# Up products on 384 tokens, with a PSUM bank for each half, in the last two sequences of an attention and mixture kernel

## The chip, the cores and the metric

The kernel runs on one core of a Trainium2 chip. The metric is the device time of one execution in microseconds (us); the time before is 678.16 us, the median of three runs (678.03 to 678.35). The engines named below are PE (TensorE, the matrix multiplier; PEld is its weight load, which runs beside the multiplying), DVE (VectorE), ACT (ScalarE), POOL (GpSimd) and SP (SyncE, which here only issues DMAs).

## What is computed

A local attention with summary keys feeds a gated projection. Cut to what matters:

```python
# q, k, v: (4 sequences, 8 heads, 768 tokens, 64); all float32
k_sum = k.reshape(B, H, 24, 32, D).max(axis=3)
v_sum = v.reshape(B, H, 24, 32, D).mean(axis=3)
scores_l = q @ k^T / 8, kept where |i - j| < 16, else -1e9
scores_s = q @ k_sum^T / 8 + log(32)
a = softmax(concat(scores_l, scores_s))
x = (a @ concat(v, v_sum))            # 3072 tokens x 512
out = ((x @ w_a) * (x @ w_b)) @ w_out # w_a, w_b: 512 x 1536, w_out: 1536 x 512
```

## The kernel before

**The projection.** The 1536 hidden columns are 12 blocks of 128 (index `f`), and the 3072 tokens are 12 chunks of 256 (index `u`, three to a sequence). One pair of a chunk and a block is an item (`item`, L1001): 144 items in all. To keep float32 accuracy every operand is held as a high and a low part, and a product is three products of parts (high with high, high with low, low with high). So the up product of one half (`up`, L981; half a with `w_a`, half b with `w_b`) is 4 slices of the 512 inputs times 3 part pairs, 12 matmuls with 128 x 128 weights standing in the array and 256 tokens of x streaming (L987). An item has 24 of them. Then a chain of four short steps: ACT copies half a out of PSUM (`g`, L1013), DVE multiplies half b by it (L1016), ACT rounds the product to its high part (`gh`, L1018), DVE subtracts that to get the low part (`gl`, L1021). The down product (`down`, L1027, matmuls L1031) then takes `gh` and `gl` as weights, 128 tokens at a time, with 512 columns of `w_out` streaming: for each of the chunk's two token tiles two matmuls with `gh` and one with `gl`, 6 per item, summed over f in the banks o0 and o1.

**PSUM.** There are 8 banks of 512 float32 columns. Both halves of an item share one bank, 256 columns each, and items alternate between h0 and h1 (`pa, pb = bank[hk][:, :CH], bank[hk][:, CH : 2 * CH]`). o0 to o3 hold outputs, c0 and c1 serve the attention. After the third chunk, o2 and o3 also serve the attention, and its token tiles alternate between (c0, c1) and (o2, o3) (L914 and L915).

**The attention.** It runs beside the projection, two chunks ahead, one tile of 128 tokens at a time (`attention`, L908): scores on PE (L617), mask and row maximum on DVE (L642, L650), exponentials on ACT (L662), normalisation on POOL (L692), twelve 32 x 256 transposes on DVE (L736), the product with the values on PE (L750), and a split of the result into the high and low part of x on ACT (L758) and DVE (L761). Per sequence, `prep_keys` (L486) builds the keys and `prep_values` (L528) the value summaries: loads of v, adds on POOL (L545), and small DMAs that put the sums into another layout (`S<-S` in the trace) and from there beside the values (`vw<-S`). The value product of a sequence's first tile needs them.

**Order.** Nothing loops at run time. Every operation is entered into `Work` (L44) with a rank, a duration and what it reads and writes; `emit` (L74) walks through modelled time and writes each engine's program in the resulting order: of the operations whose inputs are there, the one of lowest rank. `ORDER` (L23) corrects ranks and start times by the number of the operation, for operations 3 to 626. Each engine then runs its program strictly in that order and waits on semaphores. The down product of an item has the rank n - 0.5, so that it comes after the up product of the next item where its inputs are not there earlier. The four chain steps have the rank 0 and come first where they are ready.

Of the kernel before, what the change touches and what calls it, by code (L numbers as in the profile page):

```python
# [9 lines left out]
F32 = mybir.dt.float32  # L10
F32R = mybir.dt.float32r
# [97 lines left out]
def attention_moe(  # L109
# [10 lines left out]
    nc = tc.nc  # L120
# [11 lines left out]
    NR = S // CH  # L132
    NU = NR * B
    G = CH // P
    CV = 512
# [70 lines left out]
    xs = [[sb([P, NP, CH], f"x{i}_{p}", F32R) for p in range(2)] for i in range(2)]  # L206
    gs = [sb([P, CH], f"g{i}") for i in range(2)]
    ghs = [sb([P, CH], f"gh{i}", F32R) for i in range(2)]
    gls = [sb([P, CH], f"gl{i}", F32R) for i in range(2)]
# [9 lines left out]
    spaces = {n: sb([P, 2048], n) for n in ("S0", "S1")}  # L219
# [4 lines left out]
    kins = [kin, spaces["S1"][:, 2 * CV : 2 * CV + S + 32]]  # L224

# [40 lines left out]
    def rank_of(u):  # L266
        return FIRST if u == 0 else NEXT if u < FILL else SOON if u == FILL else LATER
# [134 lines left out]
    vsums = {}  # L402

# [7 lines left out]
    def blocks(rank, key, dst, x, b, c, row, more=()):  # L411
# [6 lines left out]
        for h in range(2):  # L418
            for e in range(D // 32):
# [6 lines left out]
                for rows, m in spans:  # L426
                    load(
                        rank, 4 * m, 95, more, [f"{key}.{r0}"],
# [57 lines left out]
    def prep_keys(b):  # L486
        rank = PREP
        work.add("-", 0, 0, 0, (), ["S1.2", "S1.3"], lambda: None)
        more = ["done12"], ["S1.2", "S1.3"]
        for c in range(NP):  # L490
            kw = kins[c % 2]
            keys = blocks(96, f"kin{c % 2}", kw, k, b, c, -16, more[c % 2])
# [35 lines left out]
    def prep_values(b):  # L528
# [3 lines left out]
        rank = LATER  # L532
        vs, vk = slot("S0", 2)
        work.add("-", 0, 0, 0, (), [vk], lambda: None)
        vs = vsums[b] = vs[:NS].rearrange("p (h d) -> p h d", d=D)

        vm, pk = spaces["S1"][: 4 * NS, 4 * CV - D :], "vm"
        work.add("-", 0, 0, 0, ["S1.3"], [pk], lambda: None)
        x = spaces["S1"][: 4 * NS, : 2 * T * D]
        keys = ["S1.0", "S1.1"]  # L540
# [7 lines left out]
        for hg in range(2):  # L548
            vv = v[b, 4 * hg : 4 * hg + 4].rearrange("h (n t) d -> (h n) t d", t=BLK)
            for i in range(BLK // T):  # L550
                load(
                    100, 197.0, 150, (), [keys[i % 2]],
                    slot("S1", i % 2)[0][: 4 * NS].rearrange("p (t d) -> p t d", d=D),
                    vv[:, i * T : (i + 1) * T, :],
                )
                if i % 2:
                    n = T * D
# [3 lines left out]
                    if i == 1:  # L561
                        add(n, vm, x[:, :n], x[:, n : 2 * n], keys + [pk])
                    else:
                        add(n, x[:, :n], x[:, :n], x[:, n : 2 * n], keys)
                        add(n, vm, vm, x[:, :n], keys + [pk])
            pool(
                rank, 0.3, (), [pk],
                lambda: nc.gpsimd.tensor_scalar(
                    out=vm, in0=vm, scalar1=1.0 / BLK, scalar2=None, op0=ALU.mult
                ),  # L570
            )
            for h in range(4):
                load(
                    99, 6.0, 20, [pk, vk], [f"{vk}.{hg}.{h}"],
                    vs[:, 4 * hg + h, :], vm[h * NS : (h + 1) * NS, :],
                )
        return [f"{vk}.{hg}.{h}" for hg in range(2) for h in range(4)]
# [15 lines left out]
    def scores(u, t, qT, qk, s, sk, banks, diag=None, lead=None):  # L593
        kind = 0 if t == 0 else 2 if t == S // P - 1 else 1
        rank = rank_of(u) + (0.2 * (t % G) if u < FILL else 0)
# [42 lines left out]
        for h in range(2):  # L638
            if not masked:
# [14 lines left out]
        for h in range(2):  # L654
            l = m[:, 1, h, :]
# [42 lines left out]
    def transposes(u, t, s, sk, banks, diag=None):  # L698
        rank = rank_of(u)
# [28 lines left out]


        for i, kb in enumerate(((0, 1, 3), (1, 2, 3), (0, 1, 2), (1, 2, 3))):  # L730
            qs = slice(32 * i, 32 * (i + 1))
            for j in kb:
                js = slice(32 * j, 32 * (j + 1))
                dve(
                    rank, 0.45, sk + ["S0.2"] * own, [f"{key}{i}{j}"],
# [412 lines left out]
```

## Time and profile before

| what | value |
|---|---|
| median of 3 runs | 678.16 us (678.03 to 678.35) |
| the profiled execution's own time | 678.28 us |
| its span, first to last instruction | 676.5 us |
| outside the span | 1.8 us |
| PE busy | 657.0 us, 97% of the span |
| DVE busy | 434.4 us, 64% |
| ACT busy | 255.4 us, 38% |
| POOL busy | 186.8 us, 28% |
| granted TensorE clock, mean | 0.999 of full speed (2.4 GHz) |

The profile is of one execution. A busy share tells how much of the span an engine had work in flight, and a busy PE is not yet a PE at its best rate: matmuls overlap in the pipeline, so the rate is read from the distance between the starts of successive groups, not from the duration of one. Idle time of an engine counts only where PE waits for it. In slices of one fortieth of the span (16.9 us) DVE is busy 7 to 9 tenths in the first 330 us and 2 tenths in the last 100 us, PE 9 tenths in all slices but the first three and the last.

### The profile page before, as it was taken

The numbers are of one execution on the slowest core, as the hardware profiler recorded it, in microseconds if no ns is written. First come the engines' busy times: TensorE is split into PE (matmuls) and PEld (weight loads), VectorE is DVE, ScalarE is ACT, GpSimd is POOL, SyncE is SP. The second block draws the span as 40 slices with busy tenths as digits, with TensorE's granted clock in tenths as the row PEclk, the third lists the DMA queues.
The fourth block names the chain that finished last, engine by engine and source line by source line (L and its number), as shares of the span: only waits on it lengthen the run. The fifth ranks groups of instructions, "written<-read, shape, count | busy, mean of one in ns | idle before, by whom it ended". The sixth has DMA issues, their size and how long they took to land.

```text
span 676.5 us, 15121 instructions
## 1 busy us (share of the span) xinstructions
PE 657.0 (97%) x5988; PEld 620.7 (92%) x5988; DVE 434.4 (64%) x989; ACT 255.4 (38%) x797; POOL 186.8 (28%) x231
## 2 busy tenths in 40 slices
PE   6889999999999999999999999999999999999997
PEld 4679989899999999999999999999999999999996
DVE  4799999996757768777665776762772762322222
ACT  4996665533323333234332332332332432211211
POOL 6678979851533310413110101110110110000000
PEclk9999999999999999999999999999999999999999
DMA  9999863266224135532311330310310100000000
GB/s 226 264 284 238 266 169 126 41 137 137 67 78 112 49 56 103 96 61 80 57 25 28 75 57 15 77 25 1 87 25 1 56 22 1 33 1 1 32 1 32
DMA packets 155087, 54.84 MB, mean 81 GB/s; under 512 B 132472, under 2 KB 148088, under 8 KB 155016
## 3 DMA queue, kind: packets, MB, share of 16 engines
q1 hardware_dynamic: 154872, 53.74, 33.5%
q8 instruction: 47, 0.77, 0.5%
q14 instruction: 24, 0.20, 0.1%
q10 hardware_dynamic: 144, 0.13, 0.1%
HBM read 47.12 MB, written 6.29 MB: 79 GB/s over the span
## 4 chain that ended last, share of the span: by engine, by line
PE 77%; DVE 11%; SPq 3%; ACT 3%; issue 2%; DMA 2%; POOL 1%; DVEq 0%; ACTq 0%; POOLq 0%
PE h L987 47%; PE o L1031 23%; SPq L260 3%; DVE c L339 2%; PE c L750 2%; PE c L617 2%; PE o L750 1%; DVE pt L736 1%; ACT s L662 1%; DVE space L345 1%; PE o L617 1%; DVE S L345 1%; DVE space L332 1%; DMA space<-in_v_dram 1%; DVE S L332 1%
## 5 line engine op out<-in xcount | busy, mean ns | idle before, releaser
L987 PEld LDWEIGHTS h<-x,w 128*128 128x128 f32 x3456 | 405.0, 192 | 6.8 <-DVE x L761 0.6
L987 PE MATMUL h<-x,w 128*128 128x256 f32 x3456 | 406.7, 275 | 0.3 <-DVE x L761 0.3
L1016 DVE TENSOR_TENSOR h<-h,g 128x256 f32<-128x256 f32 x144 | 61.9, 430 | 148.9 <-ACT g L1013 147.6
L1031 PE MATMUL o<-w,gh 128*128 128x512 f32 x576 | 151.8, 386 | 1.4 <-ACT gh L1018 1.3
L1013 ACT COPY g<-h 128x256 f32<-128x256 f32 x144 | 53.6, 372 | 256.4 <-PE h L987 256.3
L1031 PEld LDWEIGHTS o<-w,gh 128*128 128x128 f32 x576 | 103.6, 197 | 12.1 <-ACT gh L1018 2.6
L692 POOL TENSOR_TENSOR s<-s,nml 128x512 f32<-128x512 f32 x40 | 41.6, 1041 | 233.1 <-DVE nml L677 232.6
L736 DVE STREAM_TRANSPOSE pt<-s 32x256 f32<-32x256 f32 x228 | 99.4, 436 | 7.1 <-POOL s L692 2.0
L1031 PE MATMUL o<-w,gl 128*128 128x512 f32 x288 | 86.3, 381 | 0.0
L1021 DVE TENSOR_TENSOR gl<-h,gh 128x256 fp32r<-128x256 f32 x144 | 60.4, 419 | 30.6 <-ACT gh L1018 29.3
L662 ACT ACTIVATE s<-s,nml 128x128 f32<-128x128 f32 x160 | 62.2, 391 | 44.9 <-DVE nml L650 44.9
L1018 ACT CAST gh<-h 128x256 fp32r<-128x256 f32 x144 | 53.5, 371 | 65.3 <-DVE h L1016 65.1
L1031 PEld LDWEIGHTS o<-w,gl 128*128 128x128 f32 x288 | 55.9, 196 | 6.1 <-issue 0.3
L545 POOL TENSOR_TENSOR S<-S 96x64 f32<-96x64 f32 (+3 forms) x54 | 35.2, 651 | 41.6 <-DMA S<-in_v_dram 30.7
L324 ACT ACTIVATE c<-raw 128x512 f32<-128x512 f32 x36 | 26.9, 748 | 13.1 <-DVE S L332 6.6
L662 ACT ACTIVATION_READ_ACCUMULATOR s<-s,nml 128x1 f32 x160 | 30.1, 188 | 0.0
L382 POOL TENSOR_TENSOR space<-space,w 128x1024 f32<-128x1024 f32 (+1 forms) x14 | 26.8, 1915 | 8.8 <-ACT w L377 6.6
L671 DVE TENSOR_SCALAR nml<-nml 128x4 f32<-128x4 f32 x40 | 9.6, 243 | 28.4 <-ACT s L662 28.4
L388 POOL TENSOR_TENSOR w<-space 128x1024 fp32r<-128x1024 f32 (+1 forms) x14 | 26.7, 1912 | 1.0
L650 DVE TENSOR_REDUCE nml<-s 128x4 f32<-128x512 f32 x40 | 25.3, 667 | 0.0
L444 POOL COPY kT<-ksum 128x144 f32<-128x144 f32 x16 | 4.7, 308 | 62.8 <-DVE ksum L522 48.0
L382 POOL TENSOR_TENSOR S<-S,w 128x512 f32<-128x512 f32 (+1 forms) x11 | 17.4, 1582 | 6.4 <-ACT w L377 6.4
(109 smaller groups left out, 460.6 us busy)
## 6 DMA issues: line engine op xcount, KB each, us to landing
raw<-in_moe_w_a_dram SPq DMA_DIRECT2D x12, 512.0 KB
raw<-in_moe_w_b_dram SPq DMA_DIRECT2D x12, 512.0 KB
raw<-in_moe_w_out_dram SPq DMA_DIRECT2D x12, 512.0 KB
out_dram<-S SPq DMA_DIRECT2D x23, 256.0 KB
qin<-in_q_dram SPq DMA_DIRECT2D x160, 32.0 KB
S<-in_v_dram SPq DMA_DIRECT2D x24, 192.0 KB
vw<-in_v_dram SPq DMA_DIRECT2D x18, 192.0 KB
kin<-in_k_dram SPq DMA_DIRECT2D x24, 100.0 KB
```

Of the source, the lines that this page charges most:

```text
L324: nc.scalar.activation(bank["c0"], high[:, :, 1].bitcast(F32), AF.Prelu, scale=2.0**-112, alpha=-(2.0**32))
L382: lambda ms=ms, f8=f8: nc.gpsimd.tensor_tensor(out=f8, in0=f8, in1=parted(0)[:, ms].bitcast(F32), op=ALU.subtract),
L545: lambda: nc.gpsimd.tensor_tensor(out=out, in0=i0, in1=i1, op=ALU.add),
L662: lambda h=h, c=c, sums=sums: nc.scalar.activation(s[h][:, c, :], x[h][:, c, :], AF.Exp, bias=m[:, 0, h, c : c + 1], scale=1.0, accum_out= ...
L692: lambda h=h, r=r: nc.gpsimd.tensor_tensor(out=s[h], in0=s[h], in1=r[:, :, None].broadcast_to([P, NP, P]), op=ALU.mult,),
L736: lambda js=js, qs=qs: nc.vector.transpose(out=pv[js, :, qs], in_=sv[qs, :, js]),
L987: nc.tensor.matmul(ps, w[:, c, part, :], x[xpart][:, c, :].rearrange("p (a b) -> p b a", a=G), start=(i == 0), stop=(i == n - 1),)
L1013: act(CHAIN, 0.38, [hk], [gk], lambda: nc.scalar.copy(out=g, in_=pa))
L1016: lambda: nc.vector.tensor_tensor(out=pa, in0=pb, in1=g, op=ALU.mult),
L1018: act(CHAIN, 0.41, [hk], [ghk], lambda: nc.scalar.copy(out=gh, in_=pa))
L1021: lambda: nc.vector.tensor_tensor(out=gl, in0=pa, in1=gh.bitcast(F32), op=ALU.subtract),
L1031: nc.tensor.matmul(bank[ok[j]], (gh if first else gl)[:, j::G], w[:, :, part, :].rearrange("p (z a) n -> p z n a", a=2), start=(f == 0 and ...
```

## The change

The chunks of the third and fourth sequence become 384 tokens (`WIDE = 3` tiles of 128), two to a sequence instead of three: 10 chunks instead of 12. In these chunks

- an up matmul streams 384 columns instead of 256;
- half a fills the bank h0 and half b the bank h1, and the two halves are two entries of the plan instead of one; the chain multiplies into half b's bank; there is one buffer of `g`, `gh`, `gl` of 384 columns instead of two of 256;
- a down product covers three tiles: 9 matmuls into o0, o1 and o2. The attention therefore keeps c0 and c1 for scores and o3 for value products, from the second sequence on;
- q is loaded a tile at a time (4 DMAs of half the size per tile instead of 16 per two tiles).

In all chunks x now lies in one tile of 9 slots (`xt`), stored so that the matmul's interleaved read steps by 64 columns instead of 128; the split (L802 and after) reads PSUM with a step of 2 for it, and `gh` and `gl` are read as weights without a step. The value sums of a sequence have their own small tile (`vm`); those of the third and fourth sequence are prepared from one buffer instead of two. Ranks after the third chunk go by sequence and tile. In the very last item half b of the up product is placed between the two parts of the previous item's down product.

```diff
-    NR = S // CH
-    NU = NR * B
+    WIDE = 3
+    chunks = [(b, t, n) for b, n in enumerate((G, G, WIDE, WIDE)) for t in range(0, S // P, n)]
+    NU = len(chunks)
...
-    xs = [[sb([P, NP, CH], f"x{i}_{p}", F32R) for p in range(2)] for i in range(2)]
+    xt = sb([P, 9, NP, P], "x", F32R)
...
+    vm = sb([P, 2, D], "vm")
...
-    def rank_of(u):
-        return FIRST if u == 0 else NEXT if u < FILL else SOON if u == FILL else LATER
+    def rank_of(u, t=None):
+        if u > FILL:
+            b, t0, _ = chunks[u]
+            return LATER + 2 * b + 0.2 * (t0 if t is None else t)
+        return FIRST if u == 0 else NEXT if u < FILL else SOON
...
+        at, keys, rank = (0, ["S1.0", "S1.1"], LATER) if b == 1 else (3, ["S1.3"], 50)
...
-                    100, 197.0, 150, (), [keys[i % 2]],
+                    90, 197.0, 150, (), [keys[j]],
...
-        if u > FILL:
-            banks, vbank = [["c0", "c1"], ["o2", "o3"]], ["c0", "o2"]
+        banks, vbank = ["c0", "c1"], ["c0", "c1"] if u == FILL else ["o3"] * n
...
-                    x[xpart][:, c, :].rearrange("p (a b) -> p b a", a=G),
+                    inputs_of(u, xpart)[:, :, c].rearrange("p g (a b) -> p g b a", a=2),
...
+            W = m * P
+            ghk, glk = "gh0", "gl0"
+            pa, pb, g, gh, gl = bank["h0"][:, :W], bank["h1"][:, :W], gt[:, :W], ght[:, :W], glt[:, :W]
+            for nm, ps, hk in (("a", pa, "h0"), ("b", pb, "h1")):
+                pe(
+                    n - (1.45 if n == total - 1 and nm == "b" else 0), 12 * (0.112 if m == 2 else 0.163), xk + weight_key(f, nm), [hk],
+                    lambda nm=nm, ps=ps: up(nm, f, u, ps),
+                )
+            act(CHAIN, 0.13 + W / 1030, ["h0"], ["g0", "g1"], lambda: nc.scalar.copy(out=g, in_=pa))
+            dve(
+                CHAIN, 0.08 + W / 1000, ["g0", "h1"], ["h1"],
+                lambda: nc.vector.tensor_tensor(out=pb, in0=pb, in1=g, op=ALU.mult),
+            )
+            act(CHAIN, 0.16 + W / 1030, ["h1"], [ghk], lambda: nc.scalar.copy(out=gh, in_=pb))
...
-                        bank[ok[j]], (gh if first else gl)[:, j::G],
+                        bank[ok[j]], (gh if first else gl)[:, j * P : (j + 1) * P],
```

**Where the order moves.** Up to the score product of the second sequence's first tile, the five engines' programs have the same order. Three places after that follow. In them h_75 and h_76 are the banks h0 and h1, o_71 to o_74 the banks o0 to o3, c_77 and c_78 the attention's banks, a name w with a number is a slot of weights, and x2 or x12 is the count of equal instructions in a row.

PE in the third sequence, an item in the steady state; before, the up product of one item and the down product of the item ahead of it (the 24 up matmuls of an item are rows like the first three, and here are its last):

```order
L987 MATMUL h_75<-x_0_171,w_1477 128x256 x2
L987 MATMUL h_75<-x_1_172,w_1477 128x256
L987 MATMUL h_75<-x_0_171,w_1477 128x256
L1031 MATMUL o_71<-w_1384,gh_176 128x512 x2
L1031 MATMUL o_72<-w_1384,gh_176 128x512 x2
L1031 MATMUL o_71<-w_1384,gl_178 128x512
L1031 MATMUL o_72<-w_1384,gl_178 128x512
```

and after:

```order
L1037 MATMUL h_76<-x,w_558 128x384 x12
L1037 MATMUL h_75<-x,w_665 128x384 x12
L1108 MATMUL o_71<-w_558,gh 128x512 x2
L1108 MATMUL o_72<-w_558,gh 128x512 x2
L1108 MATMUL o_73<-w_558,gh 128x512 x2
L1108 MATMUL o_71<-w_558,gl 128x512
L1108 MATMUL o_72<-w_558,gl 128x512
L1108 MATMUL o_73<-w_558,gl 128x512
L1037 MATMUL h_76<-x,w_665 128x384 x12
```

Between an item's half b (bank h1) and its down product now stands half a of the next item, 12 matmuls, where the 24 matmuls of a whole item stood.

SP, from the loads of q for the second sequence's tiles 2 and 3 to the value sums of that sequence; before:

```order
L260 DMA qin<-in_q_dram 32x8x32 x16
L260 DMA S_187<-in_v_dram 96x512 x4
L260 DMA S_186<-S_187 24x64 x4
L260 DMA vw_165<-S_186 24x512
L260 DMA vw_166<-S_186 24x512
```

and after:

```order
L288 DMA S_181<-in_v_dram 96x512 x3
L288 DMA qin<-in_q_dram 32x8x32 x9
L288 DMA S_181<-in_v_dram 96x512
L288 DMA qin<-in_q_dram 32x8x32 x7
L288 DMA S_182<-vm 24x64 x4
L288 DMA vw_165<-S_182 24x512
L288 DMA S_181<-in_v_dram 96x512
L288 DMA vw_166<-S_182 24x512
```

The last loads of v for this sequence went ahead of the loads of q, and a load for the third sequence stands in the middle of them. On PE the value product that reads `vw` stood behind the up product of the tenth hidden block of the third chunk; it now stands earlier, between the high and the low part of the down product of the seventh block, with one more score product (of tile 2) ahead of it.

PE, the end of the program; before:

```order
L987 MATMUL h_76<-x_0_171,w_1614 128x256
L1031 MATMUL o_71<-w_1558,gh_175 128x512 x2
L1031 MATMUL o_72<-w_1558,gh_175 128x512 x2
L1031 MATMUL o_71<-w_1558,gl_177 128x512
L1031 MATMUL o_72<-w_1558,gl_177 128x512
L1031 MATMUL o_71<-w_1614,gh_176 128x512 x2
L1031 MATMUL o_71<-w_1614,gl_178 128x512
L1031 MATMUL o_72<-w_1614,gh_176 128x512 x2
L1031 MATMUL o_72<-w_1614,gl_178 128x512
```

and after:

```order
L1037 MATMUL h_76<-x,w_1609 128x384
L1108 MATMUL o_71<-w_1553,gl 128x512
L1108 MATMUL o_72<-w_1553,gl 128x512
L1108 MATMUL o_73<-w_1553,gl 128x512
L1108 MATMUL o_71<-w_1609,gh 128x512 x2
L1108 MATMUL o_72<-w_1609,gh 128x512 x2
L1108 MATMUL o_71<-w_1609,gl 128x512
L1108 MATMUL o_72<-w_1609,gl 128x512
L1108 MATMUL o_73<-w_1609,gh 128x512 x2
L1108 MATMUL o_73<-w_1609,gl 128x512
```

Between the last up matmul and the last down product stood 6 matmuls of the item before; now stand the 3 with its low part.

## Rows read from the trace of the kernel before

**Rows 1.** The page: span, busy time and share, chain that ended last by engine

```profile
span 676.5 us, 15121 instructions
PE 657.0 (97%) x5988; PEld 620.7 (92%) x5988; DVE 434.4 (64%) x989; ACT 255.4 (38%) x797; POOL 186.8 (28%) x231
PE 77%; DVE 11%; SPq 3%; ACT 3%; issue 2%; DMA 2%; POOL 1%; DVEq 0%; ACTq 0%; POOLq 0%
```

**Rows 2.** Stretches: length, busy us (instructions) of PE, PEld, DVE, ACT, POOL, clock, DMA

```profile
575.10:622.80 47.70, 47.70 (x361) 46.22 (x360) 11.89 (x27) 9.84 (x27) 0.00 (x0) 1.00 0.04 12
416.70:469.10 52.40, 52.40 (x490) 50.20 (x489) 29.80 (x70) 16.64 (x60) 4.17 (x4) 1.00 0.17 37
```

**Rows 3.** Timeline of one steady item: start, us, engine, line, operation, [idle before]

```profile
602.94 2.84 PE L987 MATMUL h<-x,w 128*128 128x256 f32 x24
...
605.62 1.03 PE L1031 MATMUL o<-w,gh 128*128 128x512 f32 x4
605.87 0.37 ACT L1013 COPY g<-h 128x256 f32<-128x256 f32 x1 [2.74 <-PE h L987]
...
606.28 0.43 DVE L1016 TENSOR_TENSOR h<-h,g 128x256 f32<-128x256 f32 x1 [2.68 <-ACT g L1013]
...
606.75 0.37 ACT L1018 CAST gh<-h 128x256 fp32r<-128x256 f32 x1 [0.50 <-DVE h L1016]
606.92 2.84 PE L987 MATMUL h<-x,w 128*128 128x256 f32 x24
```

**Rows 4.** Groups by line and shape: busy us, mean ns | idle before

```profile
L1016 DVE TENSOR_TENSOR h<-h,g 128x256 f32<-128x256 f32 x144 | 61.9, 430 | 148.9 <-ACT g L1013 147.6
L1018 ACT CAST gh<-h 128x256 fp32r<-128x256 f32 x144 | 53.5, 371 | 65.3 <-DVE h L1016 65.1
L642 DVE SCALAR_TENSOR_TENSOR s<-c,mask 128x512 f32<-128x512 f32 x22 | 14.3, 685 | 2.8 <-PE c L617 2.8
L758 ACT CAST x<-c 128x512 fp32r<-128x512 f32 x11 | 6.5, 590 | 1.3 <-PE c L750 1.3
L1076 ACT COPY S<-o 128x512 f32<-128x512 f32 x11 | 6.5, 590 | 13.8 <-PE o L1031 13.8
```

**Rows 5.** Timeline of a chain that met attention work on DVE

```profile
453.00 0.43 DVE L1016 TENSOR_TENSOR h<-h,g 128x256 f32<-128x256 f32 x1
...
453.47 0.37 ACT L1018 CAST gh<-h 128x256 fp32r<-128x256 f32 x1 [1.07 <-DVE h L1016]
```

**Rows 6.** Timeline around the second sequence's first value product: SP, PE, POOL

```profile
164.10 8.70 SPq L260 DMA_DIRECT2D qin<-in_q_dram  x16
...
164.50 1.10 PE L617 MATMUL o<-kT,qT 64*64 64x128 f32 x32
...
170.55 1.65 POOL L545 TENSOR_TENSOR S<-S 96x256 f32<-96x256 f32 x3
...
184.33 3.40 SPq L260 DMA_DIRECT2D S<-S  x4
...
188.23 2.84 PE L987 MATMUL h<-x,w 128*128 128x256 f32 x24
...
189.06 1.51 SPq L260 DMA_DIRECT2D vw<-S  x2
...
191.97 1.04 PE L750 MATMUL c<-pt,vw 128*64 128x64 f32 x28 [0.36 <-DMA vw<-S]
```

**Rows 7.** Timeline of the end

```profile
670.88 0.71 PE L1031 MATMUL o<-w,gh 128*128 128x512 f32 x2
...
672.10 0.38 PE L1031 MATMUL o<-w,gl 128*128 128x512 f32 x1
...
672.51 0.37 ACT L1053 COPY S<-o 128x256 f32<-128x256 f32 x1 [0.27 <-PE o L1031]
672.73 0.98 SPq L1064 DMA_DIRECT2D out_dram<-S  x2
```

**Rows 8.** GB/s moved by the DMAs in 40 slices of 640 to 677 us

```profile
GB/s 0 0 0 0 0 0 0 18 0 0 0 0 0 0 0 0 0 0 0 0 0 0 0 0 0 0 18 0 0 0 0 0 0 0 0 0 266 301 0 0
```

More of the change, by code (lines that the diff above doesn't have):

```diff
@@ L224, in attention_moe, with homes_of, inputs_of, summed @@
     kins = [kin, spaces["S1"][:, 2 * CV : 2 * CV + S + 32]]
+    late = []
+    def homes_of(u):
+        n = chunks[u][2]
+        if u <= FILL:
+            return [[f"X{u % 2 * 2 * G + p * G + i}" for i in range(n)] for p in range(2)]
+        if u % 2:
+            return [[f"X{6 + i}" for i in range(n)], [f"S0.{i}" for i in range(n)]]
+        return [[f"X{p * WIDE + i}" for i in range(n)] for p in range(2)]
+    def inputs_of(u, part):
+        names = homes_of(u)[part]
+        if names[0][0] == "X":
+            i = int(names[0][1:])
+            return xt[:, i : i + len(names)]
+        if not late:
+            late.append(wp.tile([P, 4, NP, P], F32R, tag="S0", name="late"))
+        return late[0][:, : len(names)]
+    def summed(b):
+        x = spaces["S0"][:NS, 2 * CV : 3 * CV] if b == 1 else spaces["S1"][4 * NS : 5 * NS, 3 * CV :]
+        return x.rearrange("p (h d) -> p h d", d=D)
     def slot(space, i):
@@ L773, in attention_moe @@
     VK = [f"v{i}" for i in range(5)]
+    VS = [f"vs.{h}" for h in range(H)]
     s0 = [sbuf[:, h] for h in range(2)]
@@ L935, in begin @@
-            scores(
-                u, t0 + i, qTs, "qT", s0, SK, banks[i], lead=lead.pop() if lead else None
-            )
+            keys = list(qk)
+            if n != G:
+                for c in range(NP):
+                    keys += blocks(
+                        98, f"q{(t0 + i) % 2}.{c}", qin[:, c, place(i)], q, b, c, (t0 + i) * P, (),
+                        old if chunks[u - 1][2] == G and i < 2 else (),
+                    )
+            dve(
+                rank_of(u, t0 + i) - 0.05 * (u > FILL), 0.62, keys, ["qT"],
+                lambda: nc.vector.transpose(out=qTs, in_=qin[:, :, place(i)]),
+            )
@@ L971, in attention @@
                 turned(i)
-                lead.append(products(*end(i)))
+                if u == FILL + 1:
+                    values(*end(i))
+                else:
+                    lead.append(products(*end(i)))
         if u == NU - 1:
@@ L1018, in item @@
-        act(CHAIN, 0.41, [hk], [ghk], lambda: nc.scalar.copy(out=gh, in_=pa))
-        dve(
-            CHAIN, 0.34, [hk, ghk], [glk],
-            lambda: nc.vector.tensor_tensor(
-                out=gl, in0=pa, in1=gh.bitcast(F32), op=ALU.subtract
-            ),
-        )
-        ok = [f"o{2 * (u == 1) + j}" for j in range(2)]
-        def down(first, banks=range(2)):
+        g, gh, gl = gs[i], ghs[i], gls[i]
+        xk = [x for names in homes_of(u) for x in names]
+        m = chunks[u][2]
@@ L1028, in down @@
+        def down(first, banks=range(m)):
             w = weight(f, "o")
```

207 lines of the change are left out of this document (117 added, 90 removed).

## The prediction

> **What bounds the kernel now.** First the page: PE is busy for 97% of the span, and 77% of the chain that ended last is PE [rows 1]. A busy PE may still wait inside its pipeline, so the next view is the stretches of the second half. From 575.10 us there is no attention left, and 12 items take 47.70 us; from 416.70 us the same 12 items, with two tiles of attention between them, take 52.40 us, that is 2.3 us for a tile's value and score products and nothing for waiting; DVE, ACT and POOL are far from full, and the granted clock is 1.00, the level of 2.4 GHz, throughout [rows 2]. The timeline of one item shows why nothing else counts there: the up product starts at 602.94, the down product at 605.62, the next up product at 606.92 [rows 3]. So 24 up matmuls take 2.68 us, 111.7 ns each, 6 down matmuls 1.30 us, 216.7 ns each, and the item 3.98 us. The chain of ACT and DVE between them ends long before PE asks for its result. What changes PE's own time in these two sequences changes the end, as long as the waits stay hidden.
>
> **The change, part by part.** The sum is made against the profiled execution's own 678.28 us, 0.12 us above the median of the three runs.
>
> *Wider up matmuls.* In the last two sequences 72 items with 24 up matmuls each, 1728, become 48 items with 24 each, 1152; the columns streamed are the same. The price of a 384-column matmul is in no row. At 2.4 GHz 256 columns are 106.7 ns and 512 are 213.3 ns, so the rows' 111.7 and 216.7 ns hold an excess of 5.0 and 3.4 ns [rows 3]. One end: 384 columns cost three quarters of the wide matmul, 162.5 ns; the other: 160 ns plus the narrow one's excess, 165.0 ns. I take the wide matmul's excess, 163.4 ns: PEld, which loads weights beside the matmuls, is busy for 46.22 of 47.70 us [rows 2], which suggests that the narrow matmul's larger excess comes from weights that barely keep up, and at 384 columns they have half as much time again. That gives 1728 x 111.7 = 193.0 us before and 1152 x 163.4 = 188.2 us after: 4.7 us less, between 2.9 (576 matmuls fewer at 5.0 ns) and 5.8. The down product keeps its count, 18 matmuls per 768 tokens and block, and its price.
>
> [...]
>
> *The chain with one bank for each half.* Half a's copy now runs under half b. After half b remain: 0.25 us until the first step starts (605.62 to 605.87), the multiplication, the rounding, and about 0.05 us between steps [rows 3]. DVE takes 430 ns for 256 and 685 ns for 512 columns, ACT 371 and 590 [rows 4]; halfway, 384 columns are 0.56 and 0.48 us. So `gh` is there 1.4 us after half b, and half a of the next item covers 12 x 163.4 ns = 1.96 us: a margin of 0.56 us. Before, the chain of 1.55 us stood against 2.68 us, a margin of 1.13. The low part needs 0.6 us more and has the high part's six matmuls, 1.3 us, as cover. What stands queued behind a late `gh` is the down product, then half b of the next item. The longest delay that I see in the rows, an ACT rounding that waited 1.07 instead of 0.50 us because DVE was on transposes [rows 5], is 0.57 us, just the new margin. I enter 0; without the cover it is a rival below.
>
> *x stored another way.* The split now reads PSUM with a step of 2. ACT's output copy does that already and takes 590 ns, as the split does [rows 4]: 0. The streamed x steps by 64 columns instead of 128; no row has that step, and I enter 0.
>
> *Banks and order of the second sequence.* Value and score products are as many as before; one pair more is taken apart, 0.1 us. The waits move. Before, the second sequence's first value product found its summaries late: the up product ahead of it started at 188.23 and let PE go at 190.91, and 28 of its 32 products started only at 191.97, after the DMA; 0.9 us lost [rows 6]. Now it stands earlier. From 164.4 us, where the orders part, PE has four up products (10.7 us), two whole down products (2.6), two score products (2.4) and parts of down products (2.2) ahead of it, and arrives at 182.3. SP starts its 16 loads of q at 164.10 as before, 8.7 us; one load of v in their middle waits for POOL's three adds after 170.55, which end at 172.2, 3 to 4 us of standstill with its own issue; then the four summary DMAs, 3.4 us, their landing, 1.3 us (187.73 to 189.06), the two `vw` DMAs and the load between them, 2.0 us, and 1.4 us until they have landed (190.57 to 191.97) [rows 6]. That is 184.5: a wait of 2.2 us, 1.3 us more than before. It could be gone altogether (0.9 us less than before) or 3 us.
>
> *The end.* Before, the last `gh` had 6 matmuls of the item ahead as cover, 1.30 us against 1.55, and PE stood for 0.25 us until 670.88 [rows 7]. Now the cover is three, 0.65 us, against 1.4: 0.5 us more. Then the last outputs: 512 KB went out in two slices of 0.925 us at 266 and 301 GB/s [rows 8]; now it is 768 KB, 0.9 us more at that rate, of which an earlier start of the first tile gives some back: 0.5. Together 1.0 us, between 0.5 and 1.4.
>
> **Sum**: -4.7 + 0.1 + 1.3 + 1.0 = -2.3 us, 676.0 us for a profiled execution, 675.9 us beside the median.
>
> **The rivals.** *A: the excess belongs to each matmul, not to the weights.* Then 576 fewer matmuls give 2.9 us, and 677.7 us remain, no change that can be measured (0.2%, 1.4 us, is about what can be told apart). For it: the excess is nearly as large at 512 columns, where weights have ample time. Against it: it falls from 5.0 to 3.4 ns. [...]
>
> *B: the chain comes out of its cover, slower than before.* The place is the down product's wait for `gh` in the 384-token chunks. It decides at a delay of 0.56 us: DVE transposes (0.57 us of delay in rows 5) and an ACT exponential in the same chain would give about 1.0, 0.4 us of standing PE. If 12 of the 48 items meet that, 4.8 us are lost: 680.7 us. For it: eight tiles of attention run in these chunks. Against it: the same meetings leave PE unbroken now, and the chain steps go first where they are ready.
>
> *C: the value product isn't late*, since the order was planned for its data to be there: 2.2 us less, 673.7 us.
>
> *D: the change doesn't do what it says, because the 64-column step slows the stream.* One ns per 256 columns in the 10 chunks from the first on is 3.5 us: 679.4 us.
>
> **How the numbers follow.** Forecast 0.50 (its own range 674.5 to 677.2), A 0.17, B 0.12, C 0.14, D 0.05, something else 0.02. Faster by over 0.2% (below 676.8): 0.44 of the forecast, C, and 0.04 of A, 0.62. Within 0.2%: 0.06 of the forecast, 0.13 of A, 0.04 of B and D, 0.23. Slower: 0.15. For the range 673.3 to 679.3 I leave out most of B, the tail of C below its 673.7 and part of D.
>
> **What would show it.** In the timeline of a pure stretch of the last chunk: from one half a to the next down product 1.96 us, an item 5.87 us; over 1.98 us speaks for A, and 2.68 us of a narrow up product in the second sequence excludes D. Idle time of PE and PEld before the down product, put down to ACT's `gh`, is B; the same before the value product near 182 us, put down to the DMA into `vw`, is my third term, and none there is C. The gap before the last down product should be 0.75 us. I'd be wrong if the attention, now with one set of score banks, made PE wait at score products where it never did.

## The result and the profile after

The changed kernel takes 671.93 us (median of 4 runs, 671.64 to 672.07) against 678.10 us for the kernel before (4 runs, 677.95 to 678.35): a ratio of 0.991, interval 0.989 to 0.993. The forecast was 675.9 us with a range from 673.3 to 679.3. The sign was right, but 6.2 us were gained, not 2.3, and the time lies under the range.

The page of the changed kernel answers to [rows 1]; its lines are the span and the busy time of the engines:

```profile
span 670.4 us, 14057 instructions
PE 651.5 (97%) x5412; PEld 608.5 (91%) x5412; DVE 429.7 (64%) x940; ACT 250.6 (37%) x751; POOL 191.1 (29%) x255
```

The span fell by 6.1 us and PE's busy time by 5.5, with 576 matmuls fewer. PE is as full as it was.

The timeline of one steady item of the last chunk (start, us, engine, line, operation, idle time before it) answers to [rows 3]:

```profile
602.48 0.33 PE L1037 MATMUL h<-x,w 128*128 128x384 f32 x1
...
604.70 0.56 DVE L1094 TENSOR_TENSOR h<-h,g 128x384 f32<-128x384 f32 x1 [3.80 <-PE h L1037]
...
605.30 0.48 ACT L1096 CAST gh<-h 128x384 fp32r<-128x384 f32 x1 [4.03 <-DVE h L1094]
...
606.38 1.46 PE L1108 MATMUL o<-w,gh 128*128 128x512 f32 x6
...
608.32 0.33 PE L1037 MATMUL h<-x,w 128*128 128x384 f32 x1
```

24 up matmuls (half b of one item, then half a of the next) run from 602.48 to 606.38: 3.90 us, 162.5 ns each, where the forecast took 163.4. Nine down matmuls take 1.94 us, from 606.38 to 608.32, 215.6 ns each, where it took 216.7. The chain is as foreseen: 0.56 us on DVE, 0.48 us on ACT, and `gh` is ready at 605.78, 0.60 us before PE wants it (forecast 0.56).

The second sequence's first value product answers to [rows 6]. SP's queue, POOL and PE between 159 and 185 us:

```profile
161.02 1.89 SPq L288 DMA_DIRECT2D S<-in_v_dram  x3
165.37 4.27 SPq L288 DMA_DIRECT2D qin<-in_q_dram  x9
169.87 0.32 SPq L288 DMA_DIRECT2D S<-in_v_dram  x1
170.23 3.38 SPq L288 DMA_DIRECT2D qin<-in_q_dram  x7
173.72 3.49 SPq L288 DMA_DIRECT2D S<-vm  x4
178.51 0.71 SPq L288 DMA_DIRECT2D vw<-S  x1
180.06 0.75 SPq L288 DMA_DIRECT2D vw<-S  x1
...
167.18 1.04 POOL L722 TENSOR_TENSOR s<-s,nml 128x512 f32<-128x512 f32 x1 [0.39 <-DVE nml L707]
168.18 1.26 POOL L570 TENSOR_TENSOR S<-S 96x256 f32<-96x256 f32 x2
169.80 3.02 POOL L570 TENSOR_TENSOR S<-S 96x512 f32<-96x512 f32 x4
173.29 0.37 POOL L595 TENSOR_SCALAR vm<-vm 96x64 f32<-96x64 f32 x1
...
176.21 2.84 PE L1037 MATMUL h<-x,w 128*128 128x256 f32 x24
178.89 1.03 PE L1108 MATMUL o<-w,x 128*128 128x512 f32 x4
...
182.53 1.15 PE L783 MATMUL o<-pt,vw 128*64 128x64 f32 x32
```

All 32 value products run in one piece from 182.53, with no wait. PE's arrival was forecast at 182.3. The load of v in the middle of the loads of q (169.87) takes 0.32 us and stands for nothing. 24 up matmuls of 256 columns take 2.68 us, as before (176.21 to 178.89). In the kernel before, the same product met a second wait ahead of the one in [rows 6], and the two add up to 0.57 us:

```profile
191.28 0.34 PE L750 MATMUL c<-pt,vw 128*64 128x64 f32 x4 [0.21 <-DMA vw<-S]
```

The end answers to [rows 7]:

```profile
662.21 0.81 PE L1108 MATMUL o<-w,gl 128*128 128x512 f32 x3
663.61 1.13 PE L1108 MATMUL o<-w,gh 128*128 128x512 f32 x4 [0.59 <-ACT gh L1096]
...
665.44 0.38 PE L1108 MATMUL o<-w,gl 128*128 128x512 f32 x1
```

The gap before the last down product is 0.75 us (662.86 to 663.61), as forecast. From the last matmul's start to the end of the span it is 4.96 us now (665.44 to 670.4) and was 4.40 (672.10 to 676.5 [rows 1, 7]).

**How the runs are compared.** In some executions the granted clock fell below 1 for a while between 20 and 60 us (0.87 to 0.96 there in the profiles that show it), and all that follows comes up to 4 us later, so what is read below is the stretch from the second sequence's first score product to the end of the span. The changed kernel was profiled again beside the experiments; this is its row for 20 to 60 us, with the clock, 0.91, third from the end:

```profile
20.00:60.00 40.00, 35.07 (x370) 30.80 (x371) 32.61 (x66) 32.33 (x92) 25.48 (x20) 0.91 1.09 269
```

> The changed kernel itself, on the chip on which the others run, to have its time and its trace beside theirs: 671.9 us as before on another chip, if the chips agree.

Measured: 673.64 us (6 runs, 671.94 to 675.67), ratio 0.990 (0.988 to 0.993). In the profiled execution the second sequence's first score product starts at 164.19 instead of 160.62, 3.57 us later, and all 17 later score products are 3.56 or 3.57 us later too. So in this pair what stands behind that point repeated to 0.01 us, and below single profiles are compared there. The spans are given to 0.1 us, so the last two columns are no finer than that. For the whole kernels:

| kernel | first score product of the second sequence, us | span, us | from there to the end, us | against the changed kernel |
|---|---|---|---|---|
| before | 160.67 | 676.5 | 515.8 | +6.0 |
| changed | 160.62 | 670.4 | 509.8 | 0 |
| changed, again | 164.19 | 673.9 | 509.7 | -0.1 |
| e1_ranks | 164.61 | 675.9 | 511.3 | +1.5 |
| e2_layout | 162.73 | 673.8 | 511.1 | +1.3 |
| e4_end | 160.60 | 671.0 | 510.4 | +0.6 |
| e6_tail | 161.03 | 670.0 | 509.0 | -0.8 |
| e8_narrow | 161.05 | 675.6 | 514.6 | +4.8 |
| e8_step | 160.16 | 675.4 | 515.2 | +5.5 |
| e10_ranks_alone | 160.68 | 683.2 | 522.5 | +12.7 |
| e11_loads | 161.68 | 676.2 | 514.5 | +4.7 |

### The profile page after: what moved, and what is told of

The parts are those of the page before. It is cut to its first block, busy times and chain, and to the rows that moved or that the text cites. A ratio compares the mean times of both kernels' runs of the same rounds, so it can differ in the third digit from the quotient of the medians.

```text
span 670.4 us, 14057 instructions
## 1 busy us (share of the span) xinstructions
PE 651.5 (97%) x5412; PEld 608.5 (91%) x5412; DVE 429.7 (64%) x940; ACT 250.6 (37%) x751; POOL 191.1 (29%) x255
## 4 chain that ended last, share of the span: by engine, by line
PE 76%; DVE 14%; DMA 3%; issue 3%; ACT 2%; SPq 2%; POOL 0%; DVEq 0%; ACTq 0%
PE h L1037 46%; PE o L1108 23%; PE o L783 3%; PE c L643 3%; DVE c L370 2%; DVE space L376 1%; SPq L288 1%; DMA raw<-in_moe_w_out_dram 1%; DVE space L363 1%; DVE S L376 1%; DVE pt L767 1%; DVE S L363 1%; DVE h L1072 1%; ACT s L692 1%; DMA space<-in_v_dram 1%
## 5 line engine op out<-in xcount | busy, mean ns | idle before, releaser
L1037 PE MATMUL h<-x,w 128*128 128x256 f32 (+1 forms) x2496 | 398.5, 295 | 0.3 <-DVE x L806 0.3
L1037 PEld LDWEIGHTS h<-x,w 128*128 128x128 f32 x2496 | 357.5, 191 | 5.7 <-DVE x L806 0.6
L1037 PE MATMUL h<-late,w 128*128 128x256 f32 (+1 forms) x384 | 115.4, 300 | 0.0
L1108 PE MATMUL o<-w,gh 128*128 128x512 f32 x432 | 109.0, 383 | 1.8 <-ACT gh L1074 1.3
L1094 DVE TENSOR_TENSOR h<-h,g 128x384 f32<-128x384 f32 x48 | 27.2, 566 | 113.7 <-PE h L1037 113.0
L1037 PEld LDWEIGHTS h<-late,w 128*128 128x128 f32 x384 | 73.1, 190 | 1.2
L1108 PE MATMUL o<-w,x 128*128 128x512 f32 x216 | 54.0, 384 | 0.1
L1072 DVE TENSOR_TENSOR h<-h,g 128x256 f32<-128x256 f32 x72 | 30.8, 428 | 31.3 <-ACT g L1069 30.2
L1108 PEld LDWEIGHTS o<-w,x 128*128 128x128 f32 x216 | 38.4, 189 | 6.0 <-issue 0.5
L570 POOL TENSOR_TENSOR S<-S 96x256 f32<-96x256 f32 (+3 forms) x58 | 33.2, 572 | 35.0 <-DMA S<-in_v_dram 30.3
L670 DVE SCALAR_TENSOR_TENSOR s<-c,mask 128x512 f32<-128x512 f32 x40 | 27.3, 685 | 13.4 <-PE c L643 13.4
```

Source lines behind the costliest of these rows:

```text
L570: lambda: nc.gpsimd.tensor_tensor(out=out, in0=i0, in1=i1, op=ALU.add),
L670: lambda h=h: nc.vector.scalar_tensor_tensor(out=s[h], in0=bank[banks[h]].rearrange("p (c x) -> p c x", x=P), scalar=0.125, in1=mask[:, ki ...
L1037: nc.tensor.matmul(ps, w[:, c, part, :], inputs_of(u, xpart)[:, :, c].rearrange("p g (a b) -> p g b a", a=2), start=(i == 0), stop=(i == n ...
L1072: lambda: nc.vector.tensor_tensor(out=pa, in0=pb, in1=g, op=ALU.mult),
L1094: lambda: nc.vector.tensor_tensor(out=pb, in0=pb, in1=g, op=ALU.mult),
L1108: nc.tensor.matmul(bank[ok[j]], (gh if first else gl)[:, j * P : (j + 1) * P], w[:, :, part, :].rearrange("p (z a) n -> p z n a", a=2), st ...
```

## The experiments

**What an up matmul costs by its columns.** Two kernels run the up products of the wide chunks on fewer columns and leave the rest out:

```diff
+        y = 64 if chunks[u][2] == G else 44 if nm == "a" else 52
+        if y < 64:
+            ps = ps[:, : 6 * y]
...
-   inputs_of(u, xpart)[:, :, c].rearrange("p g (a b) -> p g b a", a=2),
+   inputs_of(u, xpart)[:, :, c].rearrange("p g (a b) -> p g b a", a=2)[:, :, :y],
```

The quoted expectation has the two widths the wrong way round: as the diff shows, a ran on 264 columns and b on 312.

> Leaves out part of the computation in the wide chunks of the last two sequences: each up product a runs on 312 and each up product b on 264 of the 384 columns; the rest of the columns keeps what was there. It is a look at the price of one up matmul by its columns in the steady stretches (from the starts of the 12 matmuls of a product). Theory: a matmul takes its columns at 2.4 per ns and 2.5 ns more (384: 162.5 ns, measured), and the 111.7 ns of a 256-column matmul (109.2 by that) are a floor that the load of the next weights sets: then 312 columns take 132.5 ns (1.590 us for 12) and 264 take 112.5 ns (1.350 us). Rival: price is a straight line through the two measured points, 111.7 at 256 and 162.5 at 384: then 133.9 ns (1.607 us) and 114.9 ns (1.378 us). The whole kernel is near 672 - 48 x (3.90 - 2.95) = 626 us by either, if nothing else ends last.

> Leaves out part of the computation in the wide chunks of the last two sequences: each up product a runs on 240 and each up product b on 204 of the 384 columns. Under 256 columns the two prices part most. Theory (the load of the next weights sets a floor near the 111.7 ns of a 256-column matmul): 12 matmuls of either product take 1.33 to 1.34 us (111 to 112 ns each), although their columns alone would be 100.0 and 85.0 ns. Rival (columns at 2.4 per ns and a fixed few ns): 102.5 to 105 ns for 240 (1.23 to 1.26 us) and 87.5 to 91 ns for 204 (1.05 to 1.09 us).

Here y was 40 for a and 34 for b. Timeline of PE in a steady stretch of the first of the two, with 312 and 264 columns:

```profile
588.46 0.30 PE L1040 MATMUL h<-x,w 128*128 128x312 f32 x1
...
589.92 0.41 PE L1040 MATMUL h<-x,w 128*128 128x312 f32 x2
590.16 0.28 PE L1040 MATMUL h<-late,w 128*128 128x264 f32 x1
...
591.29 0.28 PE L1040 MATMUL h<-x,w 128*128 128x264 f32 x1
```

The same view of the second, with 204 and 240 columns:

```profile
582.05 0.39 PE L1040 MATMUL h<-x,w 128*128 128x204 f32 x2
...
583.06 0.40 PE L1040 MATMUL h<-x,w 128*128 128x204 f32 x2
...
583.41 0.39 PE L1040 MATMUL h<-x,w 128*128 128x240 f32 x2
...
584.41 0.28 PE L1040 MATMUL h<-x,w 128*128 128x240 f32 x1
```

Eleven matmuls of 312 columns lie between 588.46 and 589.92: 132.7 ns each. Ten of 264 lie between 590.16 and 591.29: 113.0 ns. Nine of 204 lie between 582.05 and 583.06: 112.2 ns; nine of 240 between 583.41 and 584.41: 111.1 ns. With 256 columns it was 111.7 [rows 3], with 384 it is 162.5. So from 264 columns up the price is the columns at 2.4 per ns and 2.5 to 3 ns (110.0, 130.0 and 160.0 ns of columns), and below it stays at 111 to 112 ns, down to the 204 columns tried: the straight line (133.9 and 114.9, or 105 and 91 ns) is refuted. The 256-column matmul of the kernel before stood on that floor. That the load of the next weights sets the floor would fit, but PEld's busy share doesn't show it: it was 46.22 of 47.70 us there [rows 2], and in the changed kernel, where the columns set the pace, it is 14.49 of 15.00 us (580 to 595 us). No run changed the load of the up products, and a fixed cost of each pair of a load and a matmul would look the same. So the floor is shown, its cause is not.

The Trainium skill, page "TensorE: Matmul & The Clock Gate", section "Back-to-back issue gap", gives N / 2.4 + 2.5 ns at the full clock as the gap of a single matmul by itself; of a stream of weight loads and matmuls, which these kernels are, it says that both set the spacing, and that the formula is too low at small N and too high at large N (131 ns measured at 512). The traces agree with the formula at 312 and 384 columns (132.5 and 162.5) and nearly at 264 (112.5). At 256, 240 and 204 columns it gives 109.2, 102.5 and 87.5 and is too low, as the page says for small N; at 512 the 215.6 ns here are near the formula's 215.8 and far from 131.

The whole kernels took 644.62 and 635.29 us, one run each, where 626 had been written for the first. One part of the miss is the chain: half a of the next item covers only 12 x 113 ns, 1.36 us, in the first, and 12 x 111, 1.34 us, in the second. The groups by line and shape show what PE waited for ahead of the down products; first the one with 264 and 312 columns:

```profile
L1111 PE MATMUL o<-w,gh 128*128 128x512 f32 x432 | 113.2, 393 | 6.5 <-ACT gh L1099 5.0 <-ACT gh L1077 1.3
```

And the one with 240 and 204:

```profile
L1111 PE MATMUL o<-w,gh 128*128 128x512 f32 x432 | 113.2, 393 | 10.0 <-ACT gh L1099 8.7 <-ACT gh L1077 1.3
```

5.0 and 8.7 us for `gh` of wide items (line 1099 in these two), against 0.6 us in the changed kernel, all of it at the end. Nine down matmuls also take longer, 2.05 us in the first (591.45 to 593.50) where they took 1.94; the rest of the miss I left open. So rival B's mechanism exists; with 1.95 us of cover it costs nothing, with some 1.35 it does.

**The down product's weights.** The down products read `gh` and `gl` with a step again, and the output rows are written with it:

```diff
-   bank[ok[j]], (gh if first else gl)[:, j * P : (j + 1) * P],
+   bank[ok[j]], (gh if first else gl)[:, j::m],
```

> The changed kernel, but each down product reads its weights (the hidden values gh and gl) with a step of m columns (m = 2 in chunks of 256 tokens, 3 in chunks of 384) in place of 128 columns in a row, and the rows of the output are written with that step, so that the result is the same. All else stays. Theory: reading weights with a step costs the load about 8 ns (197 against 189) and the matmul behind it about 1 ns, so nine down matmuls of a wide item take 1.950 us again (216.7 ns each) in place of 1.942, and six of a narrow one 1.300; 864 down matmuls are there, some 700 of them back to back: 672.4 to 672.8 us. Rival: the step is free, and nine in a row are only cheaper than six because a change of kind costs something once: 1.942 us stay, 671.9 +- 0.2.

Measured: 674.56 us (6 runs, 673.04 to 677.35), ratio 0.994 (0.992 to 0.996); 1.3 us more from the second sequence on. The group of the down products' weight loads between 580 and 640 us, where all items are wide (busy us, mean ns), here:

```profile
L1108 PEld LDWEIGHTS o<-w,gh 128*128 128x128 f32 x66 | 14.2, 255 | 0.0
```

And in the changed kernel:

```profile
L1108 PEld LDWEIGHTS o<-w,gh 128*128 128x128 f32 x60 | 11.1, 189 | 1.1
```

The step is not free, though the loads lie beside the matmuls. In the wide chunks, with a step of 3, the loads take 255 ns, more than the expected 197; in the narrow ones, with a step of 2, they take 197 (170 to 300 us). Score products that stood 2.12 us behind the changed kernel's at 180 us stand 2.35 us behind at 355 us (narrow items, step 2), and the span ends 3.4 us behind (mostly wide items, step 3): about 1.0 ns for each down matmul at a step of 2 and 2.4 at a step of 3.

The cleaner test has all chunks at 256 tokens, once with weights in a row, once with the step of 2 of the kernel before. The edit is `enumerate((G, G, G, G))` in the table of chunks, and for the second one the step above.

> The changed kernel with the width alone undone: all four sequences in chunks of 256 tokens, with the new storage of x, gh and gl, the new order in the second sequence and the new places. Its end is that of the kernel before (one narrow last item). Theory: 24 more narrow items in place of the wide ones give back 5.8 us (72 x 24 x 111.7 ns against 48 x 24 x 162.5 ns), and the end's 1.06 us go, so 671.9 + 5.8 - 1.1 = 676.6 us, 1.5 us under the kernel before: 0.9 of it stands at the second sequence's first value product, 0.6 at the down products' weights. Rival: those two did not come from order and storage but from the wide chunks themselves; then the time is the kernel before's, 678.1 us.

> As the run with all chunks at 256 tokens in the new storage, but each down product reads its weights with a step of two columns as in the kernel before, and the rows of the output are written with that step. Theory: 0.9 ns for each of 864 down matmuls, 0.5 to 0.8 us over that run, and weight loads of 197 ns in place of 189. Rival: none, since the loads lie beside the matmuls: 0 +- 0.1 us in the trace.

Measured: 677.70 us (10 runs, 677.04 to 680.73), ratio 0.998 (0.996 to 1.000), and 677.87 us (10 runs, 677.13 to 681.54), ratio 1.000 (0.998 to 1.002). The medians can't tell them apart, nor either from the kernel before beyond doubt; from the second sequence on the traces can: 514.6 and 515.2 us, against 515.8 before and 509.8 changed. So the time does not show the expected 676.6 us, nor the 0.5 to 0.8 us between the two; their parts are in the traces:

- order and places alone (before to e8_step): 0.6 us less. All of it lies between 160.7 and 367 us: score and value products there lead the kernel before by 0.51 us at first and 1.14 us at the end, and from 367 to 542 us the lead stays at 1.14 to 1.15 us, so equal items cost the same. It is the size of the two waits of the kernel before, 0.57 us; e8_step has no wait of PE from 155 us on.
- weights in a row instead of a step of 2 (e8_step to e8_narrow): 0.7 us less (515.24 to 514.55). The distance between the two falls evenly, from 0.89 us at the second sequence's first score product to 0.39 at 542 us: 0.50 us for some 85 items of six down matmuls, 1.0 ns for each.
- width and end (e8_narrow to changed): 4.8 us less, which is the 5.8 of the up products less the 1.06 of the end.

**Why the first value product found its means.** First VectorE's order half by half was undone, in the second sequence:

```diff
-            if u > FILL:
+            if u > FILL and chunks[u][0] > 1:
                 rank = rank_of(u, t) - 0.1 + 0.02 * h
```

> The changed kernel with one part undone, in the second sequence only: VectorE again does the mask of both halves of a tile's scores and then both maxima, not half by half; the planner moves the loads on SP a little with it (the loads of v for the means then stand between the q loads again). Theory: in the changed kernel the second sequence's first value product met no wait because the first half's maximum, and with it ScalarE's exponentials and GpSimd's multiplies, came earlier, so that GpSimd's adds freed the buffer of v before SP got there. Then here GpSimd's first multiply of the sequence ends later by 0.6 us or more, SP stands at a v load again, and the first value product waits 0.5 to 2.2 us for the means: 672.4 to 674.1 us. Rival: the new order of the loads alone, with all loads of q issued at 0.47 us each, took the wait away. Then there is no wait over 0.1 us and the time stays at 671.9 +- 0.3.

Measured: 674.87 us (6 runs, 673.98 to 677.57), ratio 0.994 (0.992 to 0.996), and 1.5 us more from the second sequence on. Timeline of PE, POOL and SP there:

```profile
185.77 0.34 PE L783 MATMUL o<-pt,vw 128*64 128x64 f32 x4 [0.58 <-DMA vw<-S]
186.83 1.04 PE L783 MATMUL o<-pt,vw 128*64 128x64 f32 x28 [0.72 <-DMA vw<-S]
...
172.33 1.04 POOL L722 TENSOR_TENSOR s<-s,nml 128x512 f32<-128x512 f32 x1 [1.06 <-DVE nml L707]
...
178.42 0.37 POOL L595 TENSOR_SCALAR vm<-vm 96x64 f32<-96x64 f32 x1
...
175.54 0.39 SPq L288 DMA_DIRECT2D S<-in_v_dram  x1
...
178.81 3.52 SPq L288 DMA_DIRECT2D S<-vm  x4
```

The wait is back, 1.30 us. This execution runs 3.99 us behind the changed kernel's by then. Take that off, and POOL's second multiply starts at 168.34 instead of 167.18 and the mean is ready 1.14 us later; the copies S<-vm on SP start when it is, in both kernels (178.79 and 178.81 here, 173.66 and 173.72 there). So POOL's adds, queued behind the multiplies, set the time at which the copies can start. SP did not stand at a load of v, as had been written: 175.54 follows right on the load of q before it.

Then the loads of v for the means got their rank behind the loads of q back, one number:

```diff
                 load(
-                    90, 197.0, 150, (), [keys[j]],
+                    100, 197.0, 150, (), [keys[j]],
```

> The changed kernel with one number undone: the loads of v that feed the means get back their rank behind the loads of q (100 in place of 90; q has 98, the means' copies 99). The planner then sends both tiles' 16 loads of q ahead of the loads of v on SP and moves GpSimd's adds behind them. Theory: the second sequence's first value product meets no wait in the changed kernel because loads of v go ahead of and among the loads of q, which gives GpSimd something to add between the first tile's multiplies and the second's; with the old rank the means are ready several us later, PE waits for them at the first value product by 2 us or more, 674 to 682 us. Rival: VectorE's order half by half alone is what made the means early; then no wait over 0.5 us stands there and the time is 671.9 +- 0.5.

Measured: 677.88 us (10 runs, 676.45 to 679.49), ratio 0.999 (0.998 to 1.000); 4.7 us more from the second sequence on. Its timeline of SP, and of PE at the first value product:

```profile
166.42 7.73 SPq L288 DMA_DIRECT2D qin<-in_q_dram  x16
...
184.05 9.26 SPq L288 DMA_DIRECT2D qin<-in_q_dram  x16
...
196.07 1.48 SPq L288 DMA_DIRECT2D vw<-S  x2
...
198.22 0.34 PE L783 MATMUL o<-pt,vw 128*64 128x64 f32 x4 [0.38 <-DMA vw<-S]
199.07 1.03 PE L783 MATMUL o<-pt,vw 128*64 128x64 f32 x28 [0.52 <-DMA vw<-S]
```

The loads of q of one tile now stand ahead of the loads of v, and those of the next tile ahead of the last two copies of the means, so that the `vw` DMAs come 16.5 us later than in the changed kernel when the two traces are laid over each other (196.07 less 1.06, against 178.51). The wait itself is only 0.90 us, less than the 2 us expected, because the planner put the value product later on PE as well. Of the rest of the 4.7 us, 0.53 stand ahead of it, where a score product waits for DVE's transposed q, and 1.24, 0.33 and 0.59 us behind it, where PE waits for DVE; some 1.1 us I did not take apart. One rank of one kind of load is worth 4.7 of the 6.0 us here. That doesn't make it the source of the gain: with all the new order and places, but narrow chunks, 0.6 us are gained against the kernel before, which has the old rank too.

Last, the half-by-half order alone was put into the kernel before (the same two lines in its `scores`).

> The kernel before with one part of the change alone: from the second sequence on, VectorE does the mask and the maximum of one half of a tile's scores before those of the other half; the planner moves a few loads on SP with it (one load of v less ahead of the means' copies). Theory: GpSimd's multiplies of the second sequence's first tile end about 1 us earlier, its adds follow, and the first value product's waits of 0.21 and 0.36 us go: 0.5 to 0.9 us less from there on, 677.2 to 677.6 us. Rival: the loads of v still stand behind 16 loads of q there, so GpSimd waits for them as before and nothing moves: 678.1 us.

Measured: 684.79 us (6 runs, 681.97 to 685.15), ratio 1.007 (1.005 to 1.010), slower where 0.5 to 0.9 us less was expected. Its timeline, with the loads of v on SP that held the means up and the first value product on PE:

```profile
173.24 12.16 SPq L260 DMA_DIRECT2D S<-in_v_dram  x3
...
192.47 0.34 PE L754 MATMUL c<-pt,vw 128*64 128x64 f32 x4 [1.39 <-DMA vw<-S]
193.22 1.28 PE L754 MATMUL c<-pt,vw 128*64 128x64 f32 x28 [0.42 <-DMA vw<-S]
194.43 2.08 PE L1035 MATMUL o<-w,gh 128*128 128x512 f32 x4
...
197.15 1.08 PE L1035 MATMUL o<-w,gh 128*128 128x512 f32 x4
```

POOL's multiplies do come earlier (167.24 instead of 169.55), but the three loads of v behind the 16 of q now take 12.16 us, where four took 7.66, since the adds that free their buffer stand behind the next tile's multiplies on POOL (179.35 and 182.00), and PE waits 1.81 us instead of 0.57. So DVE's order alone loses here, and SP's order without it lost 1.5 us in e1; in the changed kernel they come together. The planner moved other operations in each of these runs too. The other 5.5 us of this run's loss against the kernel before are in part further waits, 1.41 us in two value products for DVE's transposes and 1.21 us for `gh`, and in part the clock: behind the wait for the means the granted clock was 0.50 from 194 to 197 us in this execution, the level of 1.2 GHz, and six down matmuls took 2.72 us (194.43 to 197.15) where they take 1.30 [rows 3]. Some 1.5 us stay open.

**The end.** The last second half was put back behind the low part of the down product ahead of it (`n` for `n - 1.45` in its rank):

> The changed kernel with one part undone, at the end alone: the last item's second up product stands behind the low part of the down product before it again, not ahead of it. Theory: the three low-part matmuls (0.65 us) no longer lie beside the chain mult, cast, so TensorE's gap before the last down product grows from 0.75 to 1.4 us and the kernel by 0.65: 672.4 to 672.7 us. Rival: the end is set by the copies and the output's transfers, which would not follow: 671.9 +- 0.2.

Measured: 673.38 us (6 runs, 672.73 to 676.55), ratio 0.993 (0.991 to 0.995); every score product to 522 us within 0.02 us of the changed kernel, then 0.6 us more. Its timeline at the last down product:

```profile
664.24 1.13 PE L1108 MATMUL o<-w,gh 128*128 128x512 f32 x4 [1.24 <-ACT gh L1096]
```

The wait grew from 0.59 to 1.24 us, 0.65 as expected. Then the opposite: the last item's second half goes to the bank `c0`, and its `gh` and `gl` to two free blocks of x, so both halves can run ahead of the whole down product before:

```diff
+            if n == total - 1:
+                ghk, glk, bk, pb = "X0", "X1", "c0", bank["c0"][:, :W]
+                gh, gl = (xt[:, j].rearrange("p c x -> p (c x)")[:, :W] for j in range(2))
```

> The changed kernel with the last item's chain in places of its own: its second up product goes to the free bank c0 and its hidden values gh and gl to two free blocks of x, so that both up products can run before the down product of the item before, which then lies beside the whole chain (copy done, mult 0.57, cast 0.48 us against nine down matmuls of 1.94 us). Theory: TensorE's wait of 0.6 us (a gap of 0.75) before the last down product goes, the time falls by 0.6 to 0.75: 671.2 us. Rival: the last outputs are bound by transfers that started earlier, and the end stays: 671.9 +- 0.2.

Measured: 672.17 us (6 runs, 671.63 to 674.85), ratio 0.990 (0.988 to 0.992), and 0.8 us less than the changed kernel by the trace; between the times themselves the intervals overlap. Its timeline of PE and ACT at the end:

```profile
661.32 1.46 PE L1112 MATMUL o<-w,gh 128*128 128x512 f32 x6
662.62 0.81 PE L1112 MATMUL o<-w,gl 128*128 128x512 f32 x3
662.69 0.48 ACT L1100 CAST x<-c 128x384 fp32r<-128x384 f32 x1 [0.63 <-DVE c L1098]
663.26 2.17 PE L1112 MATMUL o<-w,x 128*128 128x512 f32 x9
```

The cast ends at 663.17, 0.09 us before PE wants it, and 18 down matmuls run without a gap. By the trace it is the fastest version here.

**The second sequence in wide chunks too**, `(G, WIDE, WIDE, WIDE)` in the table of chunks. In this version a block of x shares its place with a narrow item's hidden values, so a part of the second sequence is not what the reference has.

> The changed kernel with the second sequence, too, in two chunks of 384 tokens in place of three of 256. Theory (price by columns): its 36 narrow items of 24 up matmuls at 111.7 ns (96.5 us) become 24 wide ones at 162.5 ns (93.6 us): 2.9 us less, 669.0 us. Rival (the tiles come too late): three tiles instead of two must be through scores, softmax and value product before TensorE runs out of the twelve narrow items of the chunk before; the second sequence's first two value products stand 11.0 us apart in the changed kernel's trace (182.53 and 193.57), so a third stands near 204.6, and the narrow items last until about 200: a wait of 3 to 6 us for x, 671.5 to 675 us.

Measured: 726.76 us (6 runs, 726.08 to 729.13), ratio 1.070 (1.068 to 1.073). The longest wait of PE:

```profile
PE o L783 <- DMA vw<-S: 22.0, 2, 21.8
```

The rival's direction was right, the place wasn't: a wait of 10.7 us at a score product, put down to DVE's `nml`, and then a single one of 21.8 us for the means, whose loads of v stand one by one among 48 loads of q on SP (from 172.96 to 197.02 us, 12, 14, 12 and 10 loads of q with one load of v between them). Behind it come 9.8 us of waits for DVE's transposes and 4.2 for a load of v, and while PE stood the granted clock fell: 0.50 from 180 to 210 us, so what PE did there ran at 1.2 GHz. Keeping the second sequence narrow is worth far more here than the 2.9 us.

## Why the prediction was wrong, step by step

| term | forecast, us | measured, us | from |
|---|---|---|---|
| up matmuls | -4.7 (-2.9 to -5.8) | -5.8 | 1728 x 111.7 to 1152 x 162.5 ns |
| second sequence's first value product, with the pair | +1.4 | -0.6 | before to e8_step; 0.57 us of waits gone |
| down matmuls' weights | 0 | -0.7 | e8_step to e8_narrow |
| chain | 0 | 0 | no wait for `gh` but at the end |
| storage of x in the up products | 0 | 0 | 2.68 us for 24 narrow ones |
| end | +1.0 | +1.06 | gaps of 0.75 and 0.25 us, 4.96 and 4.40 us |
| sum | -2.3 | -6.0 | spans: -6.1 |

**The step that failed most** is the third term, "one load of v in their middle waits for POOL's three adds after 170.55". The times of POOL were carried over from the kernel before, though the new order moves what they hang on. Three loads of v now go ahead of the loads of q, DVE gives POOL its multiplies earlier (e1: 1.3 us of wait without that), and the load of v among those of q (169.87) finds its buffer free; POOL ends the mean at 173.66, when SP has just issued the last load of q (173.61). So 2.0 us were wrong here. Rival C, which had 0.14, was right on this term ("the order was planned for its data to be there"); the 0.9 us that it took back were 0.6. PE's arrival at 182.3, in the same term, was right to 0.2 us.

**The second is a size.** The up matmul was sized at 163.4 ns and measured 162.5. Rival A, an excess that belongs to each matmul, is refuted by that and by the floor at 204 to 256 columns. "Weights that barely keep up" fits the floor, but PEld's busy share, from which it was read, is as high in the changed kernel, so there was some luck in it. The reasoning also stopped halfway: if the narrow matmul is held by its weights, a wider one need owe nothing to them, and the bound of 162.5 ns was the value to take. It cost 1.1 us.

**The third was no term at all.** The change also straightens the down products' weights, and the text entered only "its price" for them: 0.7 us, 1.0 ns for each of some 700 matmuls. Those loads lie beside the matmuls and were taken to be free; they weren't quite.

What held: the chain and its margin (0.60 against 0.56 us; B refuted, though e3 and e7 show that it would come with a shorter cover), no cost of the 64-column step (D: 2.68 us for 24 narrow matmuls as before), and the end, to 0.1 us.

## What to carry to other kernels

Ask of a back-to-back matmul first whether its columns or a floor set its pace: a few widths on either side of the one in use tell it at once, and widening past that point wins what the floor had cost. When a change gives an order to a planner, trace every queue that a data path crosses in the new order, the waits on each included, and don't carry over one absolute time from the old trace; two reorderings can each lose without the other and win together. Where runs differ by an early stretch that the change doesn't touch, lay the traces over each other behind it; here that told apart 0.5 us where medians differed by more.

## What the runs showed of the hardware

A matmul with 128 x 128 weights loaded for each cost 111 to 112 ns at 204, 240 and 256 columns, 113.0 at 264, 132.7 at 312 and 162.5 at 384, all at a granted clock of 1.00. Weights read with a step took longer to load (189 ns in a row, 197 with a step of 2, 255 with a step of 3), and about 1 ns of a step of 2 and 2.4 ns of a step of 3 came through to the 216 ns matmul although the loads lie beside the matmuls. In e10_ranks_alone the granted clock was 0.50 from 194 to 197 us, after two waits of PE of 1.39 and 0.42 us, and six down matmuls took 2.72 us there instead of 1.30.
